# Attention before a routed expert layer: K turned earlier, the row maximum taken off in PSUM, half of K's copy moved to VectorE

## The chip, the cores and the metric

The kernel runs on one core of a Trainium2 chip. PE (TensorE) multiplies matrices, DVE (VectorE) and ACT (ScalarE) do elementwise work and reductions, POOL (GpSimd) issues most transfers and some elementwise work, SP (SyncE) issues others. Each engine works through its own queue in program order and waits on semaphores for the others. The metric is device time in microseconds. Three runs of the kernel before took 343.34, 342.05 and 343.24 us; the median is 343.24.

## The reference

First a chunked attention: 4 batches, 8 heads, 768 positions, 64 columns a head. Each chunk of 32 queries sees 16 positions to its left, itself, 8 to its right, and 8 memory positions: 64 keys. Then a layer of 8 experts in which each row goes to its two best by noisy logits.

```python
for c in range(nc):
    k_full = np.concatenate([mem_k, k_ctx], axis=2)
    v_full = np.concatenate([mem_v, v_ctx], axis=2)
    scores = scale * np.matmul(q_c, k_full.transpose(0, 1, 3, 2))
    scores = scores - np.max(scores, axis=-1, keepdims=True)
    a = np.exp(scores)
    a = a / (np.sum(a, axis=-1, keepdims=True) + 1e-09)
    out[:, :, c_start:c_end] = np.matmul(a, v_full)
...
logits = x @ w_gate
noisy_logits = logits + np.log1p(np.exp(x @ w_noise)) * noise
top2 = np.argpartition(-noisy_logits, 2, axis=1)[:, :2]
...
for e in range(E):
    for k in range(2):
        mask = top2[:, k] == e
        h = np.maximum(x[mask] @ w1[e], 0.0)
        out[mask] += top2_w[mask, k, None] * (h @ w2[e])
```

Taking the row maximum off changes nothing in the quotient as long as the same value is taken off a whole row; it keeps the exponential in range.

## The kernel before

The attention works on 16 pairs of heads (`NPAIR`), one pair in one iteration of a software pipeline (lines 755 to 799). The order of work is written out by hand; nothing reorders it. In iteration i the stages of several pairs are interleaved:

- `PT_pe(i-1)` turns the exponentials P of the pair before on PE, `PT_copy(i-1)` copies them out of PSUM on ACT.
- `max_dve(i)` takes the row maxima of the scores (L288) and subtracts them into an SBUF tile (L290), both on DVE.
- `turn_pe(i+2, 0)` turns Q of a later pair on PE and copies it on ACT (L258); `turn_pe(i+2, 1)`, later in the iteration, does the same with K, whose two heads go in two copies of 64 partitions, both on ACT (L264).
- `PV_pe(i-1)` multiplies P and V on PE (L314, L317), the sums of the rows coming along as a column of ones; `mult_dve(i-1)` takes the reciprocal (L328) and writes the product (L329) on DVE.
- `exp_act(i)` takes the exponential of the subtracted scores on ACT (L295).
- `logits_pe(i-3)` and `xT_pe(i-2)` are the router's matmuls and transposes; `scores_pe(i+1)` writes the next pair's scores.

The scores have one place, two banks of PSUM (`bankS`); the value products have two more (`bankO`). The turned tiles go around three banks (`bankT`): a transpose has to wait until the copy of the tile three places before has read its bank. After every fourth pair the routing of a batch is spread over `steps(...)`: first the gate's exponential and logarithm on ACT, then small operations mostly on DVE (L369 to L470), some matmuls on PE (L407 to L412, L463, L484), one product on POOL (L456), and the gate weights' exponential on ACT (L402). DVE's queue therefore holds, in an iteration: maximum, subtraction, a routing step, reciprocal and product, another routing step. POOL issues the loads of Q and K six pairs ahead (`load_qk`) and of V three pairs ahead (`load_v`), and SP stores the rows that the router has weighted (L422). The expert work begins in the last iterations and follows until about 324 us; scatters on POOL (L676) end the kernel.

Of the kernel before, what the change touches and what calls it, by code (L numbers as in the profile page):

```python
# [12 lines left out]
F32 = mybir.dt.float32  # L13
BF16 = mybir.dt.bfloat16
F32R = mybir.dt.float32r
AX = mybir.AxisListType.X
Alu = mybir.AluOpType
Act = mybir.ActivationFunctionType
# [6 lines left out]
def kernel(  # L25
# [14 lines left out]
    nc = tc.nc  # L40
    B, H, S, D = q.shape
    n_mem = mem_k.shape[2]
    chunk, left_ctx, right_ctx = 32, 16, 8
    ncnk = S // chunk
    scale = 1.0 / math.sqrt(D)
# [6 lines left out]
    BT = S // 128  # L52
    HP = H // 2
    WIN = left_ctx + chunk + right_ctx
    CTX = WIN + n_mem
    SJ = S // 128
    assert D == 64 and CTX == 64 and 4 * chunk == 128 and S == 128 * SJ
    NPAIR = B * HP
# [20 lines left out]
    const = ctx.enter_context(tc.tile_pool(name="const", bufs=1))  # L79
# [9 lines left out]
    def body():  # L89
        actx = ExitStack()  # L90
        ap_ = actx.enter_context(tc.tile_pool(name="ap", bufs=2))
# [4 lines left out]
        bankS = psA.tile([128, 2, 512], F32, name="bankS")  # L96
# [49 lines left out]
        identb = const.tile([128, 128], BF16, name="identb")  # L146
# [21 lines left out]
        for hh in range(2):  # L168
            nc.gpsimd.dma_start(
                out=memv[64 * hh + WIN:64 * hh + CTX, :, hh, 0:D],  # L170
                in_=bass.AP(mem_v.tensor, mem_v.offset + hh * n_mem * D, [[D, n_mem], [2 * n_mem * D, NPAIR], [1, D]]))
# [20 lines left out]

        ident = ap_.tile([32, 32], F32, name="ident", bufs=1)
        nc.vector.tensor_copy(ident, identb[:32, :32])
        onesb = const.tile([128, 128], BF16, name="onesb")
        nc.vector.memset(onesb, 1.0)
        neg = const.tile([128, 2, left_ctx], BF16, name="neg")
        nc.vector.memset(neg, NEG)
        mkT = ap_.tile([128, HP, B, 2, n_mem], BF16, name="mkT", bufs=1)
        nc.vector.memset(mkT, 0.0)  # L200
        kbufs = [ap_.tile([128, 2, S], BF16, name=f"kT{i}", bufs=1) for i in range(2)]
# [44 lines left out]
        st = [dict() for _ in range(NPAIR)]  # L246
        xrows = {}

        def turn_pe(n, x):
            src = qks[n][x]  # L250
            p_t = bf16v(tr(), SJ, 128)
            for j in range(SJ):
                for hh in range(2):
                    nc.tensor.transpose(out=p_t[64 * hh:64 * hh + 64, j, :], in_=src[:, hh, j * D:(j + 1) * D], identity=identb)  # L254
            p_t = p_t.rearrange("d j p -> d p j")
            if x == 0:
                dst = ap_.tile([128, 128, SJ], BF16, name="qT", bufs=2)
                nc.scalar.copy(dst, p_t)  # L258
                st[n]["qT"] = dst.rearrange("d p j -> d (p j)")
            else:  # L260

                for hh in range(2):
                    hs = slice(64 * hh, 64 * hh + 64)
                    nc.scalar.copy(kbufs[n % 2][hs, hh].rearrange("d (p j) -> d p j", j=SJ), p_t[hs])  # L264

        UB = BT // 2

        def scores_pe(n):
            b, hp = divmod(n, HP)
            qT, kT = st[n]["qT"], kbufs[n % 2]  # L270
            ps = bankS[:, :, :UB * 2 * CTX].rearrange("p x (u h c) -> p x u h c", h=2, c=CTX)
            for u in range(BT):
                nc.tensor.matmul(out=ps[:, u // UB, u % UB, :, WIN:], lhsT=qT[:, 128 * u:128 * (u + 1)], rhs=mkT[:, hp, b], start=True, stop=True)
            for c in range(ncnk):
                u, r = divmod(c, 4)
                lo = left_ctx if c == 0 else 0
                hi = WIN - right_ctx if c == ncnk - 1 else WIN
                k0 = chunk * c - left_ctx
                o = ps[32 * r:32 * r + 32, u // UB, u % UB]
                nc.tensor.matmul(out=o[:, :, lo:hi], lhsT=qT[:, chunk * c:chunk * (c + 1)], rhs=kT[:, :, k0 + lo:k0 + hi], start=True, stop=True)  # L280
                for a, z in ((0, lo), (hi, WIN)):
                    if z > a:
                        nc.tensor.matmul(out=o[:, :, a:z], lhsT=onesb[:, :chunk], rhs=neg[:, :, :z - a], start=True, stop=True)  # L283
            st[n]["ps"] = bankS[:, :, :UB * 2 * CTX].rearrange("p x (u c) -> p x u c", c=CTX)

        def max_dve(n):
            mx = ap_.tile([128, 2, BT], F32, name="mx")
            nc.vector.tensor_reduce(out=mx, in_=st[n]["ps"], axis=AX, op=Alu.max)  # L288
            sd = ap_.tile([128, 2, BT, CTX], F32, name="sd", bufs=1)
            nc.vector.tensor_tensor(out=sd, in0=st[n]["ps"], in1=mx.rearrange("p x (u o) -> p x u o", o=1).to_broadcast([128, 2, BT, CTX]), op=Alu.subtract)  # L290
            st[n]["sd"] = sd

        def exp_act(n):
            P = ap_.tile([128, BT, 2, CTX], BF16, name="P")
            nc.scalar.activation(out=P.rearrange("p u h c -> p (u h c)"), in_=st[n]["sd"].rearrange("p x u c -> p (x u c)"), func=Act.Exp, scale=scale)  # L295
            st[n]["P"] = P

        def PT_pe(n):
# [456 lines left out]
        for i in range(NPAIR + 1):  # L755
            if i + NQ < NPAIR:
                load_qk(i + NQ)
            if i >= 1:
                PT_pe(i - 1)
            if i < NPAIR:  # L760
                max_dve(i)
            if i >= 1:
                PT_copy(i - 1)
            if i + 2 < NPAIR:
                turn_pe(i + 2, 0)
            if i < NPAIR:
                steps(1)
            if i >= 1:
                PV_pe(i - 1)
            if i < NPAIR:  # L770
                exp_act(i)
            if i >= 3:
                logits_pe(i - 3)
                if (i - 3) % HP == HP - 1:
                    begin, *rest = route((i - 3) // HP)
                    begin[0]()
                    assert not pending
                    pending.extend(rest)
            if i + 2 < NPAIR:
                turn_pe(i + 2, 1)  # L780
            if i >= 1:
                mult_dve(i - 1)
            if i >= 2:
                xT_pe(i - 2)
            if i + 1 < NPAIR:
                scores_pe(i + 1)
            if 1 <= i <= NPAIR - NV:
                load_v(i + NV - 1)
            if i == 1:
                route_constants()  # L790
            if i == NPAIR - 6:
                load_w1(0)
            if i == NPAIR - 4:
                load_w1(1)
            if i == NPAIR - 2:
                load_w2(0)
            steps(1 if i < NPAIR - 2 else 2)
            if i >= NPAIR - 1:
                units(FB // 2)
# [28 lines left out]
        half = rt.tile([64, E], F16, name="half")  # L828
# [53 lines left out]
    end, past, ovc, ramp, identb, tr, bf16v, f32v, relu, hring, yring, lp, load_w1, load_w2, W1, W2 = kept  # L882


    with tc.For_i(SKIP, end, 128) as i:
# [5 lines left out]
        for t in range(NP):  # L891
# [13 lines left out]
            out=xl, out_offset=None, in_=xd, in_offset=bass.IndirectOffsetOnAxis(ap=gi[:, 0:1], axis=0),  # L905
            bounds_check=N - 1, oob_is_err=True)
        o = lp.tile([128, Dm], F32, name="o")
# [54 lines left out]
```

## Time and profile before

| | |
|---|---|
| median of three runs | 343.24 us |
| time of the profiled execution | 343.07 us |
| span from first to last instruction | 341.3 us |
| busy: PE / DVE / ACT / POOL | 274.3 / 161.2 / 149.5 / 229.3 us |
| mean granted PE clock | 0.918 |
| starts of the sixteen maxima (L288), first and last | 13.6 and 101.3 us |
| row maximum, mean (L288) | 953 ns |
| subtraction, mean (L290) | 958 ns |
| exponential, mean (L295) | 847 ns |
| half copy of K on ACT, mean (L264) | 791 ns |

Busy time is read against a stretch of the span, not against the whole: the attention stage lies between about 10 and 104 us. An engine that is busy nearly all of a stretch bounds it there; idle time of an engine that isn't the bound costs nothing. What an engine waited for stands in brackets behind a row of the order of time, with the line that released it; "issue" there is time in which nothing that the profile shows was waited for. Matmuls are pipelined, and their ends are modelled.

### The profile page before, as it was taken

What the parts mean: (1) busy time and instruction counts of PE and PEld (TensorE: products, weight loads), DVE (VectorE), ACT (ScalarE), POOL (GpSimd) and SP (SyncE); (2) the same over time, 40 slices, a digit from 0 to 9 for tenths busy, and PEclk for the clock granted to TensorE, in tenths of its full rate; (3) what the DMA queues carried; (4) which work ended last, traced back from release to release, by engine and by line L of the source; (5) the groups of instructions that cost most, each with busy time, mean ns of one, the idle gap of its engine ahead of it and who ended that gap; (6) DMA issues with size and microseconds to landing.
All of it is one profiled execution on the core that took longest, in us unless ns stands there. A gap on an engine that the chain in (4) does not pass through costs nothing. (4 is left out here: it accounts for less than half of the span.)

```text
span 341.3 us, 7625 instructions
## 1 busy us (share of the span) xinstructions
PE 274.3 (80%) x3071; PEld 174.2 (51%) x3085; DVE 161.2 (47%) x363; ACT 149.5 (44%) x295; POOL 229.3 (67%) x219
## 2 busy tenths in 40 slices
PE   0777677878548667799999999999999999999900
PEld 0656566666436555345565555555555555455400
DVE  7457659779876465222434333342332633134100
ACT  1688988878355544123343433423423333132200
POOL 8997767737443250687788887887888784848281
PEclk9969978969695999899999999999999999999965
DMA  9999999999979999469999999999999999959395
GB/s 108 161 154 187 167 161 166 212 133 194 196 143 309 398 286 203 79 103 185 247 152 198 172 240 197 239 195 194 206 160 205 216 148 157 147 74 130 40 131 70
DMA packets 99110, 60.30 MB, mean 177 GB/s; under 512 B 63488, under 2 KB 83968, under 8 KB 99072
## 3 DMA queue, kind: packets, MB, share of 16 engines
q0 software_dynamic: 82208, 49.84, 106.5%
q1 hardware_dynamic: 15792, 9.05, 9.2%
q10 hardware_dynamic: 1072, 0.88, 0.8%
q8 instruction: 26, 0.43, 0.5%
q14 instruction: 12, 0.10, 0.1%
HBM read 65.07 MB, written 23.27 MB: 259 GB/s over the span
## 5 line engine op out<-in xcount | busy, mean ns | idle before, releaser
L676 POOL DMA_INDIRECT out_dram<-ys,idx_f x40 | 62.8, 1570 | 26.6 <-issue 14.8
L648 PEld LDWEIGHTS <-w1t 128*128 128x128 bf16 x576 | 56.3, 99 | 40.4 <-issue 5.1
L604 POOL DMA_INDIRECT xl<-x_rows,idx_f x48 | 50.0, 1041 | 26.7 <-DVE hts L633 11.2
L664 PE MATMUL bankE<-w2t,htf 128*128 128x512 bf16 x278 | 65.7, 379 | 0.5
L675 DVE TENSOR_SCALAR ys<-bankE,gt 128x512 f32<-128x512 f32 (+1 forms) x32 | 21.9, 684 | 63.3 <-PE bankE L664 49.8
L648 PE MATMUL bankE<-xTf,w1t 128*128 128x416 bf16 x256 | 50.6, 339 | 0.0
L673 ACT ACTIVATE ys<-bankE,gt 128x512 f32<-128x512 f32 x24 | 16.5, 688 | 68.1 <-PE bankE L664 59.3
L134 POOL DMA_DIRECT2D vp<-in_v_dram x34 | 33.4, 989 | 15.5 <-PE bankO L317 4.3
L664 PEld LDWEIGHTS <-htf 128*128 128x128 bf16 x288 | 27.2, 98 | 28.8 <-issue 0.2
L633 DVE TENSOR_SCALAR htf<-bankE 128x416 bf16<-128x416 f32 x32 | 18.9, 591 | 26.7 <-PE bankE L648 26.7
L631 ACT ACTIVATE htf<-bankE 128x416 bf16<-128x416 f32 x32 | 16.5, 517 | 27.1 <-PE bankE L648 27.1
L264 ACT COPY kT<-bankT 64x768 bf16<-64x768 bf16 x32 | 25.3, 791 | 6.5 <-PE bankT L254 6.2
L648 PE MATMUL bankT<-xTf,w1t 128*128 128x416 bf16 x128 | 27.8, 339 | 0.2 <-DVE htf L633 0.2
L621 PE MATMUL bankT<-identb,xl 128*128 128x128 bf16 (+1 forms) x224 | 20.5, 220 | 5.7 <-DMA xl<-x_rows,idx_f 2.4
L621 PEld LDWEIGHTS <-xl 128*128 128x128 bf16 (+1 forms) x224 | 15.4, 100 | 16.2 <-issue 4.4
L664 PE MATMUL bankE<-w2t,hts 128*128 128x512 bf16 x92 | 22.7, 395 | 0.2
L288 DVE TENSOR_REDUCE mx<-bankS 128x12 f32<-128x768 f32 x16 | 15.2, 953 | 9.1 <-PE bankS L283 9.1
L314 PE MATMUL bankO<-memv,PT 128*128 128x132 bf16 x96 | 10.2, 256 | 9.5 <-ACT PT L307 9.3
L648 PE MATMUL bankE<-xTs,w1t 128*128 128x256 bf16 (+1 forms) x104 | 14.9, 283 | 2.6 <-DVE xTs L625 1.3
L456 POOL TENSOR_TENSOR col<-mm_all,tl 128x672 f16<-128x672 f16 x4 | 6.7, 1672 | 14.6 <-DVE tl L443 14.6
L329 DVE TENSOR_TENSOR xrow<-bankO,rec 128x768 bf16<-128x768 f32 x16 | 15.3, 958 | 1.9 <-DMA x_rows<-xrow 1.4
L290 DVE TENSOR_TENSOR sd<-bankS,mx 128x768 f32<-128x768 f32 x16 | 15.3, 958 | 1.8 <-DVE mx L288 0.5
(182 smaller groups left out, 453.6 us busy)
## 6 DMA issues: line engine op xcount, KB each, us to landing
w1t<-in_moe_w_dram POOLq DMA_DIRECT2D x8, 1024.0 KB, 11.3
w2t<-in_moe_w_dram POOLq DMA_DIRECT2D x8, 1024.0 KB, 10.7
out_dram<-zt SPq DMA_DIRECT2D x3, 2048.0 KB, 10.2
vp<-in_v_dram POOLq DMA_DIRECT2D x30, 168.0 KB, 8.6
qg<-in_q_dram POOLq DMA_DIRECT2D x16, 192.0 KB, 7.7
kg<-in_k_dram POOLq DMA_DIRECT2D x16, 192.0 KB, 8.2
x_rows<-xrow SPq DMA_DIRECT2D x3, 792.0 KB, 8.4
x_rows<-xrow ACTq DMA_DIRECT2D x1, 792.0 KB
```

Source lines behind the costliest of these rows:

```text
L134: nc.gpsimd.dma_start(out=vp[p0 + j:p0 + j + nj, c:c + m, hh, :], in_=bass.AP(v.tensor, v.offset + (hd * S + c * chunk + j - left_ctx) * D ...
L264: nc.scalar.copy(kbufs[n % 2][hs, hh].rearrange("d (p j) -> d p j", j=SJ), p_t[hs])
L290: nc.vector.tensor_tensor(out=sd, in0=st[n]["ps"], in1=mx.rearrange("p x (u o) -> p x u o", o=1).to_broadcast([128, 2, BT, CTX]), op=Alu.s ...
L604: nc.gpsimd.indirect_dma_start(out=xl, out_offset=None, in_=xd, in_offset=bass.IndirectOffsetOnAxis(ap=idx[:, c:c + 1], axis=0), bounds_ch ...
L621: nc.tensor.transpose(out=p_t[:, kp, :w], in_=xl[:w, kp * 64:(kp + 1) * 64].bitcast(BF16), identity=identb[:w, :w])
L631: nc.scalar.activation(out=dst, in_=src, func=Act.Relu)
L633: nc.vector.tensor_scalar(out=dst, in0=src, scalar1=0.0, scalar2=None, op0=Alu.max)
L648: nc.tensor.matmul(out=h[:, :hi - lo], lhsT=W1[e][:, kp, f * 128:(f + 1) * 128], rhs=xTs[s][:, kp, lo:hi], start=(kp == 0), stop=(kp == KP ...
L664: nc.tensor.matmul(out=y, lhsT=ht[:, f, o:o + w], rhs=W2[e][:, f, :], start=(f == 0), stop=(f == FB - 1))
L673: nc.scalar.activation(out=ys[:, :wide], in_=y[:, :wide], func=Act.Copy, scale=gate)
L675: nc.vector.tensor_scalar(out=ys[:, :wide], in0=y[:, :wide], scalar1=gate, scalar2=None, op0=Alu.mult)
L676: ins = nc.gpsimd.indirect_dma_start(out=rows, out_offset=bass.IndirectOffsetOnAxis(ap=idx, axis=0), in_=ys[:, :wide], in_offset=None, bou ...
```

## The change

The change has three parts. K of pair i+2 is turned directly behind Q, right after P's transposes, ahead of the routing step and the value products on PE. The subtraction on DVE goes: DVE writes the maximum as bf16, and behind the value products PE adds it, multiplied by a matrix with -1 on its diagonal, to the scores in PSUM (two matmuls, one a bank); the exponential then reads PSUM. For this the score matmuls open one accumulation a bank, which the two added matmuls close. And of K's two copies the first stays on ACT and the second goes to DVE. A constant, `minus`, is made once.

```diff
--- before.py
+++ after.py
@@ -192,6 +192,8 @@
 
         ident = ap_.tile([32, 32], F32, name="ident", bufs=1)
         nc.vector.tensor_copy(ident, identb[:32, :32])
+        minus = const.tile([128, 128], BF16, name="minus")
+        nc.vector.tensor_scalar(out=minus, in0=identb, scalar1=-1.0, scalar2=None, op0=Alu.mult)
         onesb = const.tile([128, 128], BF16, name="onesb")
         nc.vector.memset(onesb, 1.0)
         neg = const.tile([128, 2, left_ctx], BF16, name="neg")
@@ -259,9 +261,12 @@
                 st[n]["qT"] = dst.rearrange("d p j -> d (p j)")
             else:
 
-                for hh in range(2):
+                def half(copy, hh):
                     hs = slice(64 * hh, 64 * hh + 64)
-                    nc.scalar.copy(kbufs[n % 2][hs, hh].rearrange("d (p j) -> d p j", j=SJ), p_t[hs])
+                    copy(kbufs[n % 2][hs, hh].rearrange("d (p j) -> d p j", j=SJ), p_t[hs])
+
+                half(nc.scalar.copy, 0)
+                half(nc.vector.tensor_copy, 1)
 
         UB = BT // 2
 
@@ -270,29 +275,34 @@
             qT, kT = st[n]["qT"], kbufs[n % 2]
             ps = bankS[:, :, :UB * 2 * CTX].rearrange("p x (u h c) -> p x u h c", h=2, c=CTX)
             for u in range(BT):
-                nc.tensor.matmul(out=ps[:, u // UB, u % UB, :, WIN:], lhsT=qT[:, 128 * u:128 * (u + 1)], rhs=mkT[:, hp, b], start=True, stop=True)
+                nc.tensor.matmul(out=ps[:, u // UB, u % UB, :, WIN:], lhsT=qT[:, 128 * u:128 * (u + 1)], rhs=mkT[:, hp, b], start=(u % UB == 0), stop=False, skip_group_check=True)
             for c in range(ncnk):
                 u, r = divmod(c, 4)
                 lo = left_ctx if c == 0 else 0
                 hi = WIN - right_ctx if c == ncnk - 1 else WIN
                 k0 = chunk * c - left_ctx
                 o = ps[32 * r:32 * r + 32, u // UB, u % UB]
-                nc.tensor.matmul(out=o[:, :, lo:hi], lhsT=qT[:, chunk * c:chunk * (c + 1)], rhs=kT[:, :, k0 + lo:k0 + hi], start=True, stop=True)
+                nc.tensor.matmul(out=o[:, :, lo:hi], lhsT=qT[:, chunk * c:chunk * (c + 1)], rhs=kT[:, :, k0 + lo:k0 + hi], start=False, stop=False, skip_group_check=True)
                 for a, z in ((0, lo), (hi, WIN)):
                     if z > a:
-                        nc.tensor.matmul(out=o[:, :, a:z], lhsT=onesb[:, :chunk], rhs=neg[:, :, :z - a], start=True, stop=True)
+                        nc.tensor.matmul(out=o[:, :, a:z], lhsT=onesb[:, :chunk], rhs=neg[:, :, :z - a], start=False, stop=False, skip_group_check=True)
             st[n]["ps"] = bankS[:, :, :UB * 2 * CTX].rearrange("p x (u c) -> p x u c", c=CTX)
 
         def max_dve(n):
-            mx = ap_.tile([128, 2, BT], F32, name="mx")
+            mx = ap_.tile([128, 2, UB * 2], BF16, name="mx")
             nc.vector.tensor_reduce(out=mx, in_=st[n]["ps"], axis=AX, op=Alu.max)
-            sd = ap_.tile([128, 2, BT, CTX], F32, name="sd", bufs=1)
-            nc.vector.tensor_tensor(out=sd, in0=st[n]["ps"], in1=mx.rearrange("p x (u o) -> p x u o", o=1).to_broadcast([128, 2, BT, CTX]), op=Alu.subtract)
-            st[n]["sd"] = sd
+            st[n]["mx"] = mx
+
+        def shift_pe(n):
+
+            for x in range(2):
+                nc.tensor.matmul(out=bankS[:, x, :UB * 2 * CTX].rearrange("p (g c) -> p g c", c=CTX), lhsT=minus,
+                                 rhs=st[n]["mx"][:, x].rearrange("p (g o) -> p g o", o=1).to_broadcast([128, UB * 2, CTX]),
+                                 start=False, stop=True, skip_group_check=True)
 
         def exp_act(n):
             P = ap_.tile([128, BT, 2, CTX], BF16, name="P")
-            nc.scalar.activation(out=P.rearrange("p u h c -> p (u h c)"), in_=st[n]["sd"].rearrange("p x u c -> p (x u c)"), func=Act.Exp, scale=scale)
+            nc.scalar.activation(out=P.rearrange("p (x u) h c -> p x (u h c)", x=2), in_=bankS[:, :, :UB * 2 * CTX], func=Act.Exp, scale=scale)
             st[n]["P"] = P
 
         def PT_pe(n):
@@ -763,11 +773,13 @@
                 PT_copy(i - 1)
             if i + 2 < NPAIR:
                 turn_pe(i + 2, 0)
+                turn_pe(i + 2, 1)
             if i < NPAIR:
                 steps(1)
             if i >= 1:
                 PV_pe(i - 1)
             if i < NPAIR:
+                shift_pe(i)
                 exp_act(i)
             if i >= 3:
                 logits_pe(i - 3)
@@ -776,8 +788,6 @@
                     begin[0]()
                     assert not pending
                     pending.extend(rest)
-            if i + 2 < NPAIR:
-                turn_pe(i + 2, 1)
             if i >= 1:
                 mult_dve(i - 1)
             if i >= 2:
```

## The prediction

> **What bounds the kernel now.** I first read the page's busy slices: the attention stage (sixteen pairs of heads, about 10 to 104 us) is followed by expert work in which PE is busy nine tenths and more. The chain that ended last holds only closing scatters and says nothing of attention, so I asked for busy time in short windows. The columns are stretch, length, then busy time and instructions of PE, PEld, DVE, ACT, POOL, then granted clock, DMA share and GB/s.
>
> ```profile
> 35.00:40.00 5.00, 3.62 (x104) 2.99 (x104) 3.22 (x5) 4.65 (x7) 3.44 (x4) 1.00 1.95 168
> 76.00:82.00 6.00, 4.84 (x128) 3.82 (x130) 5.62 (x18) 4.99 (x9) 3.58 (x7) 0.90 1.11 162
> 82.00:88.00 6.00, 3.91 (x111) 3.12 (x103) 5.83 (x15) 4.61 (x7) 4.75 (x5) 0.96 1.64 225
> ```
>
> Two regimes: an iteration without routing is ACT's (4.65 of 5.00 us), one with routing on DVE is DVE's (5.62 and 5.83 of 6.00). Next the order of time in a plain iteration, and in a routing one:
>
> ```profile
> 36.12 0.87 ACT L295 ACTIVATE P<-sd 128x768 bf16<-128x768 f32 x1
> 37.30 1.60 ACT L264 COPY kT<-bankT 64x768 bf16<-64x768 bf16 x2 [0.32 <-PE bankT L254]
> 38.92 0.80 ACT L339 COPY xt<-bankT 128x768 bf16<-128x768 bf16 x1
> 39.62 0.80 ACT L307 COPY PT<-bankT 128x768 bf16<-128x768 bf16 x1
> 40.31 0.82 ACT L258 COPY qT<-bankT 128x768 bf16<-128x768 bf16 x1
> ...
> 54.20 0.24 ACT L402 ACTIVATE ge<-gd 128x48 f32<-128x48 f32 x1 [1.26 <-DVE gd L398]
> ...
> 85.26 1.75 DVE L450 TENSOR_TENSOR Rn<-rampm,slot 128x1536 f16<-128x1536 f16 x1
> 87.52 0.94 DVE L288 TENSOR_REDUCE mx<-bankS 128x12 f32<-128x768 f32 x1
> ```
>
> ACT's ring closes in 4.88 us (P's copy before this one began at 34.74, this one at 39.62). The row at 54.20 shows ACT held for a routing operand, with the exponential queued behind it. Then the groups with the prices, count | busy and mean | idle before:
>
> ```profile
> L264 ACT COPY kT<-bankT 64x768 bf16<-64x768 bf16 x32 | 25.3, 791 | 6.5 <-PE bankT L254 6.2
> L290 DVE TENSOR_TENSOR sd<-bankS,mx 128x768 f32<-128x768 f32 x16 | 15.3, 958 | 1.8 <-DVE mx L288 0.5
> L648 PE MATMUL bankE<-xTf,w1t 128*128 128x416 bf16 x256 | 50.6, 339 | 0.0
> ```
>
> and, by the order of time, the nearest small copy on DVE and one of three stalls of PE's queue that nothing in the profile explains:
>
> ```profile
> 50.63 0.32 PE L280 MATMUL bankS<-kT,qT 128*32 128x112 bf16 x11 [1.75 <-issue]
> ...
> 117.75 0.42 DVE L625 COPY xTs<-bankT 128x512 bf16<-128x512 bf16 x1 [1.21 <-PE bankT L621]
> ```
>
> **The change, part by part.** *ACT* loses 16 of 32 K copies: 16 x 0.791 = 12.7 us. The exponential reads PSUM instead of SBUF; the 48-column pair (0.206 from PSUM, 0.242 from SBUF) says no dearer. I take 0.82.
>
> *DVE* loses 16 subtractions (16 x 0.958 = 15.3 us) and gets 16 half copies of K. No row shows a 2-byte copy whose source steps over 128 elements. From below 0.42 to 0.63 us: the 512-element copy as it stands, or scaled by 768/512; from above 0.96, what DVE takes for 768 four-byte elements of PSUM. It is nearest to the latter (768 elements of PSUM that are no neighbours), so 0.95; back to back such DVE operations follow at 0.88 to 0.90. DVE's own work thus stays about equal. What the sum would be at the lower end is rival B below. The Trainium skill's page "VectorE: DVE Perf Modes" (section "What auto-detection actually checks") lets DVE move two 2-byte elements a cycle out of PSUM only where they lie side by side, and so speaks against this change: by it the copy is at its dear end and the sum is the one below. The row of 0.42, whose elements do lie side by side, agrees but can't decide for this copy.
>
> What changes more is DVE's queue. In the changed program's list of instructions, DVE's half carries one wait, on ACT, and none on PE whose transposes it reads; this is only sound if it waits for ACT's half of the same pair. So DVE stands between the maximum and reciprocal, product and routing steps until ACT is through P's copy, Q's copy and its half of K. At the start the second pair's half even lies ahead of the first maximum.
>
> *PE* gets 32 matmuls of 384 columns. One of 416 takes 0.339 from start to end, and 16 of 256 columns follow at 0.12; a pair is so 0.18 + 0.32, about 0.5 us at full clock, 0.85 to 0.95 at half. Their operand repeats each value 64 times; no row shows that at such a width; below, nothing speaks for less than 0.5, above I bound it by twice, 1.0. The nearest repeating rows (166 to 179 ns for 8 to 40 columns) show no surcharge, so 0.5. They lie behind the value products and wait for the maximum; behind them stand logits, transposes and the next scores. The scores now wait for the exponential, not for the subtraction, since it is read from their bank. Flags of the score matmuls: no price, as the value products accumulate likewise. The one new constant on DVE (a row of its size 0.27) hides in front of the first K copy, which can't start before 12.0; without that cover 0.3.
>
> K's transposes move ahead of routing matmuls, value products, logits and the exponential. Their loads are issued 0.7 us behind Q's; Q's transposes waited 0.75 for a load at 29.25, later not. With the later start below, they come at 30.1 or after: nothing, 0.5 without that cover. POOL's value load still waits for the value products; SP's row store follows the routing: no change.
>
> **The new ring.** From the start S of scores: 0.65 scores, 0.55 P transposed, 0.80 P copied, 0.05 + 0.90 value products, 0.53 shift, 0.82 exponential, 0.06, with about 0.05 of friction: 4.41 against 4.88, if DVE's maximum starts by S + 2.0. ACT's K half ends at S + 3.4, so DVE's half starts at S + 3.45, then 0.9, then 1.25 for reciprocal and product, then routing.
>
> **The start.** Old maximum 0 at 13.61. New: ACT's half for pair 1 ends at 16.1, DVE's at 17.1; maximum 18.05, shift, exponential 19.55, scores 1 at 19.6 (16.03 before). P's copy 0 goes from 19.77 to 20.8 (ACT was the brake there), K's half 3 ends at 24.0, product 25.25, the routing constants 1.3: maximum 2 at 26.55 instead of 24.75. Scores 3: 28.95 instead of 27.52, 1.4 late.
>
> **Plain iterations.** Scores 4, 5 and 6 at 33.3, 37.7 and 42.1 (32.65, 37.54, 43.47): 1.4 early.
>
> **Routing.** Iteration 6 ends with 1.75 us of routing on DVE: maximum 7 at 49.45 (51.01). There the exponential stands behind the gate weights, which stand behind K's half and 1.3 us of routing: scores 8 at 53.8 (54.23). K's half in iteration 8 waits for ACT until 57.55 though DVE was free at 56.1; then 0.9 + 1.45 + 1.25 + 1.75: maximum 9 at 62.9 (62.92). The lead is gone. Likewise maximum 11 at 73.25 (74.19), 12 at 79.1 (79.45); DVE then waits for ACT from 80.0 to 81.35; 0.9 + 2.75 + 1.25 + 1.75 + 0.6: maximum 13 at 88.55 (87.52), 1.0 late. After the table work the value products run from 91.2, scores 14 at 93.5, or 94.6 at half clock as before; the middle, and a plain ring: scores 15 at 98.4 (97.53). The last maximum follows the gate's logarithm: 101.85 (101.34). The last shift lies ahead of the first expert matmuls on PE, 0.7 between both clocks: 1.2 us late in all.
>
> **Stalls.** This sum holds no stall of PE's queue; before had three (0.71, 1.75, 0.93 by the idle ahead of their rows), which cost 1.0 + 0.7 + 1.4 = 3.1 us on those marks. Between none and all of them I take half, 1.5, since DVE's waits cover some. The expert stage hands a late start on: PE has under 2 us of any wait in one place there. Total +2.7 on the profiled execution's 343.07 (span 341.3): 345.8, and 345.9 against the median of 343.24, which lies 0.17 above it.
>
> **Rivals.** *A, ACT's relief goes through.* If DVE never makes the ring late, 12 iterations gain 0.47 each: 1.4 + 0.7 - 5.6 = -3.5, 339.6. For it: DVE is idle 19 us in this stage for PE. Against it: the ring stays free only with at most 0.76 us of routing in an iteration, and seven of twelve show 0.7 to 5. The time turns at four of twelve gaining. *B, the half copy is cheap,* 0.42 to 0.63: nine copies lie on the path (three at the start, iterations 7 to 9 and 11 to 13), 0.32 to 0.53 each, 2.9 to 4.8 us less: 341.1 to 343.0. It turns below 0.65. Against it the step of the source; for it only that both are two bytes wide. *C, PE's clock.* PE now stands idle up to 2 us ahead of the table matmuls in iterations 9 and 13; in before it ran at half clock after idle of 0.7 to 1.5 us (43, 57, 71 us). Value products and shift at half clock cost 0.65 + 0.4 each; three iterations more: 349.1. Doubled shift matmuls give about the same.
>
> **Numbers.** My forecast 0.52 (its own range 344 to 348.5), A 0.20, B 0.15, C 0.13. This measurement tells about 0.5% from no change, 1.7 us. Faster: A and a third of B, 0.25; same: the rest of B and the low fifth of mine, 0.20; slower 0.55. For 8 in 10 the range reaches from A's time to C's: 339.3 to 349.3.
>
> **What would show it.** DVE's half of K near 0.95, with DVE idle for ACT ahead of it at about S + 3.45; maximum 2 near 26.5; plain rings near 4.4; maximum 13 near 88.5; the shift pair near 0.5 with the exponential right behind. Wrong: half copies under 0.65, DVE never idle for ACT in iterations 8 and 12, or a clock below before's in the routing iterations.

## The result, and the profile after

The changed kernel took 351.97 us in the median of four runs (350.05 to 352.64), the kernel before 342.64 beside it: a ratio of 1.0269 (95% interval 1.0211 to 1.0327). A later set of runs on another chip gave 1.0325 (1.0272 to 1.0378). It is slower, by about 9 us where 2.7 were forecast, and outside the range. The profiled execution took 352.51 us (span 350.8); the first expert matmul starts at 117.19 us instead of 106.91, so all of the loss arises in the attention stage.

The new prices come first, in the groups of the changed kernel's profile (count | busy, mean ns of one | idle before).

```profile
L266 DVE COPY kT<-bankT 64x768 bf16<-64x768 bf16 x16 | 15.4, 961 | 19.7 <-ACT kT L266 19.6
L266 ACT COPY kT<-bankT 64x768 bf16<-64x768 bf16 x16 | 12.7, 795 | 1.8 <-PE bankT L256 1.8
L305 ACT ACTIVATE P<-bankS 128x768 bf16<-128x768 f32 x16 | 12.9, 809 | 19.7 <-PE bankS L299 19.5
L299 PE MATMUL bankS<-mx,minus 128*128 128x384 bf16 x32 | 9.8, 396 | 3.0 <-DVE mx L293 3.0
```

DVE's half copy of K takes 961 ns against 795 on ACT, and in all DVE stood 19.6 us idle for ACT's half of the same tile. Busy time by stretch in the changed kernel (columns as in the prediction), beside which the prediction shows the same stretches of before:

```profile
35.00:40.00 5.00, 3.58 (x105) 2.83 (x105) 3.53 (x6) 2.96 (x5) 3.76 (x5) 1.00 1.88 175
76.00:82.00 6.00, 4.06 (x106) 3.14 (x106) 5.66 (x13) 3.52 (x7) 4.02 (x5) 1.00 1.53 110
```

ACT fell from 4.65 to 2.96 us of the plain stretch, yet no engine is full there now: between 35 and 40 us PE, DVE and ACT all wait. The order of time of a plain iteration of the changed kernel says for what.

```profile
34.95 0.29 PE L278 MATMUL bankS<-mkT,qT 128*128 128x16 bf16 x6 [0.41 <-ACT P L305]
...
36.20 0.80 ACT L317 COPY PT<-bankT 128x768 bf16<-128x768 bf16 x1 [0.60 <-PE bankT L312]
...
37.58 0.80 ACT L266 COPY kT<-bankT 64x768 bf16<-64x768 bf16 x1
38.41 0.96 DVE L266 COPY kT<-bankT 64x768 bf16<-64x768 bf16 x1 [1.37 <-ACT kT L266]
38.83 0.52 PE L327 MATMUL bankO<-vp,PT 128*32 128x128 bf16 x24 [1.26 <-issue]
39.28 0.50 PE L299 MATMUL bankS<-mx,minus 128*128 128x384 bf16 x2
...
39.82 0.81 ACT L305 ACTIVATE P<-bankS 128x768 bf16<-128x768 f32 x1 [1.44 <-PE bankS L299]
...
40.68 0.29 PE L278 MATMUL bankS<-mkT,qT 128*128 128x16 bf16 x6 [0.41 <-ACT P L305]
...
45.30 0.23 PE L327 MATMUL bankO<-vp,PT 128*32 128x128 bf16 x2 [1.56 <-issue]
```

The iteration before had run from scores at 30.50 to scores at 34.95, 4.45 us, nearly the 4.41 forecast. This one has the same order, but PE stands 1.26 us in the middle of its value products, for nothing that the profile shows, and the ring takes 5.73. The next stall, 1.56, comes at 45.30 and costs more than itself, for PE runs at half speed behind it (a row of six transposes, 0.51 us at 35.59):

```profile
47.79 0.82 PE L312 MATMUL bankT<-identb,P 128*128 128x128 bf16 x6
```

A routing iteration looks like this:

```profile
58.08 0.24 ACT L412 ACTIVATE ge<-gd 128x48 f32<-128x48 f32 x1 [2.68 <-DVE gd L408]
...
59.07 0.29 PE L278 MATMUL bankS<-mkT,qT 128*128 128x16 bf16 x6 [2.32 <-ACT P L305]
...
59.91 0.80 PE L312 MATMUL bankT<-identb,P 128*128 128x128 bf16 x6
...
63.06 0.96 DVE L266 COPY kT<-bankT 64x768 bf16<-64x768 bf16 x1 [1.84 <-ACT kT L266]
...
66.66 1.84 DVE L460 TENSOR_TENSOR Rn<-rampm,slot 128x1536 f16<-128x1536 f16 x1
...
68.43 0.94 DVE L293 TENSOR_REDUCE mx<-bankS 128x12 bf16<-128x768 f32 x1
```

The exponential waits behind the gate weights until 58.23, PE therefore idles 2.32 us, and within a microsecond its transposes run at half speed (0.80 instead of 0.51). DVE's half of K waits 1.84 us for ACT, and product, routing and the next maximum queue up behind it.

The starts of some maxima, in us; "forecast" is the prediction's sum, which holds no stall:

| maximum | 2 | 7 | 9 | 11 | 13 | 15 |
|---|---|---|---|---|---|---|
| before | 24.75 | 51.01 | 62.92 | 74.19 | 87.52 | 101.34 |
| forecast | 26.55 | 49.45 | 62.9 | 73.25 | 88.55 | 101.85 |
| after | 27.32 | 54.77 | 68.43 | 79.16 | 95.19 | 110.98 |

### The profile page after: what moved, and what is told of

Read it like the earlier page. It is cut to its first block, busy times and chain, and to the rows that moved or that the text cites. A ratio compares the mean times of both kernels' runs of the same rounds, so it can differ in the third digit from the quotient of the medians.

```text
span 350.8 us, 7695 instructions
## 1 busy us (share of the span) xinstructions
PE 280.0 (80%) x3103; PEld 177.3 (51%) x3117; DVE 162.8 (46%) x364; ACT 135.5 (39%) x279; POOL 228.8 (65%) x219
## 5 line engine op out<-in xcount | busy, mean ns | idle before, releaser
L266 DVE COPY kT<-bankT 64x768 bf16<-64x768 bf16 x16 | 15.4, 961 | 19.7 <-ACT kT L266 19.6
L674 PE MATMUL bankE<-w2t,hts 128*128 128x512 bf16 x92 | 21.5, 379 | 0.2
L305 ACT ACTIVATE P<-bankS 128x768 bf16<-128x768 f32 x16 | 12.9, 809 | 19.7 <-PE bankS L299 19.5
L317 ACT COPY PT<-bankT 128x768 bf16<-128x768 bf16 x16 | 12.8, 798 | 14.5 <-PE bankT L312 14.5
L293 DVE TENSOR_REDUCE mx<-bankS 128x12 bf16<-128x768 f32 x16 | 15.2, 952 | 5.6 <-PE bankS L288 5.5
L658 PE MATMUL bankT<-xTs,w1t 128*128 128x256 bf16 (+1 forms) x88 | 14.5, 306 | 1.6 <-ACT xTs L633 1.1
```

What stands on the lines that cost most here:

```text
L658: nc.tensor.matmul(out=h[:, :hi - lo], lhsT=W1[e][:, kp, f * 128:(f + 1) * 128], rhs=xTs[s][:, kp, lo:hi], start=(kp == 0), stop=(kp == KP ...
L674: nc.tensor.matmul(out=y, lhsT=ht[:, f, o:o + w], rhs=W2[e][:, f, :], start=(f == 0), stop=(f == FB - 1))
```

## The experiments

Two theories were set against each other. **W**: DVE's half of K waits behind ACT's half and so stands ahead of product and routing in DVE's queue. **R**: the loss is in the longer ring through the one place of the scores, which now runs through PE's shift and takes in PE's stalls and its low clock. The parts are called a (K turned directly behind Q), b (the shift on PE), c (half of K's copy on DVE). The runs were made on several chips, on which the kernel before took 342.05 to 345.49 us in the median; a ratio is always to the kernel before on the same chip, while the expected times went by some 343 us.

**The third part taken back** (a and b stay).

```diff
-                half(nc.scalar.copy, 0)
-                half(nc.vector.tensor_copy, 1)
+                for hh in range(2): ... nc.scalar.copy(...)
```

> The change without its third part: both halves of K's copy on ACT, the turn ahead and the subtraction in PSUM stay. Theory W (the forecast's: DVE's half, queued behind ACT's half, makes DVE late and costs the time): the wait of 19.6 us on DVE goes, the first maximum is back near 13.8 us, plain rings lengthen from 4.45 to about 5.1 us because ACT copies 0.8 us more, routing rings shorten by 1 to 1.5 us; time 343 to 346 us. Theory R (the ring: scores, maximum, shift and exponential now follow one another through one place in PSUM, and PE's stalls and half clock lie on it): the ring stays, only the start gets better; time 348 to 351 us.

342.84 us, ratio 1.0039 (0.9996 to 1.0082), just below W's 343 to 346 and far below R's 348. Without c nothing is left of the loss that could be told from no change. The plain ring is 5.1 us. PE stalls at the very instructions of after, but for 0.18 and 0.82 us instead of 1.26 and 1.56, and once more, 0.74 us, at 82.83: with the slower ring the first two are shorter.

**The second part taken back** (a and c; the subtraction is on DVE again, the shift and its flags are gone).

```diff
+            nc.vector.tensor_tensor(out=sd, in0=st[n]["ps"], in1=mx..., op=Alu.subtract)
...
-                shift_pe(i)
```

> The change without its second part: the subtraction is on DVE again, K turned ahead and half of its copy on DVE stay. DVE then has 15.3 us of subtractions and 15.4 us of half copies. Theory W: the wait for ACT stays and DVE's load grows, slower than the changed kernel, 353 to 358 us. Theory R: scores wait for the subtraction alone, PE's stalls are absorbed again; plain rings near 4.5 us, routing rings DVE's at 6 to 6.5 us, time 344 to 349 us.

347.93 us, ratio 1.0144 (1.0057 to 1.0231): R's figure, and W's is wrong. The subtraction found room in the time in which DVE waited for ACT (that wait fell from 19.6 to 6.2 us), and from maximum 7 to 13 this kernel took 40.55 us, the changed one 40.42. So with c in place, b costs too: some 4 us, which W doesn't explain. The plain ring is 4.18 us, the fastest yet, and its stalls are the longest:

```profile
43.84 0.61 PE L340 MATMUL bankT<-identb,xrow 128*128 128x128 bf16 x4 [3.05 <-issue]
51.40 0.33 PE L283 MATMUL bankS<-kT,qT 128*32 128x112 bf16 x11 [1.11 <-issue]
65.03 0.22 PE L254 MATMUL bankT<-identb,kg 128*64 128x128 bf16 x1 [1.93 <-issue]
```

**The first part taken back** (b and c; K is turned behind the logits again).

```diff
-                turn_pe(i + 2, 1)
...
+            if i + 2 < NPAIR:
+                turn_pe(i + 2, 1)
```

> The change without its first part: K turned behind the logits again, the other two parts stay. K's copies then start later (behind the value products, as before), ACT's half behind the exponential and DVE's half behind that. Theory W: DVE stands longer for ACT, about 1 us more in each of some six rings, 354 to 360 us. Theory R: the ring is not touched by where K is turned, since the transposes fill the time in which PE waits for the exponential: 350 to 353 us. A third reading, that the transposes ahead do the harm because they need a bank that the routing still holds (2.0 us in one iteration): 347 to 350 us.

356.28 us, ratio 1.0406 (1.0321 to 1.0492). As W said: ACT's half now lies behind the exponential, so DVE waits 33.8 us for it. There is no stall of PE at rings of about 5.3.

**The third part alone.**

```diff
+                half(nc.scalar.copy, 0)
+                half(nc.vector.tensor_copy, 1)
```

> The kernel before with the third part alone: K stays turned behind the logits, the subtraction stays on DVE, and the second half of K's copy goes to DVE. W (DVE's half queues behind ACT's half and makes DVE stand in front of the product): here ACT's half lies behind the exponential, so a ring of DVE closes as maximum 0.95, subtraction 0.96, exponential 0.85, ACT's half 0.8, DVE's half 0.95, product 1.25, about 5.8 us against 4.88; over twelve iterations some 8 to 12 us are lost: 350 to 356, and DVE's wait for ACT at K's copy is above 15 us in all. R (the loss comes from the ring through the one place of the scores, which now runs through PE and stalls and a low clock stretch): nothing of that ring is here and ACT is relieved of 12.7 us, so 339 to 343.

365.42 us, ratio 1.0588 (1.0456 to 1.072): W's direction, but beyond its 350 to 356. DVE waits 24.4 us in all for ACT's half, and P's transposes wait 2.82 and 3.01 us (64.82 and 94.08 us) for a bank that DVE's late half still reads, which W hadn't counted. The ring of DVE that W worked out at 5.8 stands in the order of time of this kernel, 5.66 from maximum to maximum:

```profile
39.96 0.95 DVE L291 TENSOR_REDUCE mx<-bankS 128x12 f32<-128x768 f32 x1
...
42.68 0.78 ACT L264 COPY kT<-bankT 64x768 bf16<-64x768 bf16 x1
...
43.49 0.96 DVE L264 COPY kT<-bankT 64x768 bf16<-64x768 bf16 x1 [1.59 <-ACT kT L264]
...
45.62 0.95 DVE L291 TENSOR_REDUCE mx<-bankS 128x12 f32<-128x768 f32 x1
```

ACT lost 12.7 us of work here and the kernel became 20 us slower; c is the harmful part by itself.

**DVE's half put behind the product** (all three parts).

```diff
-                half(nc.vector.tensor_copy, 1)
+                st[n]["k1"] = lambda: half(nc.vector.tensor_copy, 1)
...
+            if i + 2 < NPAIR and i != 13:
+                st[i + 2]["k1"]()
```

> The changed kernel with DVE's half of K's copy issued behind the product of its iteration (in the last iteration but two it stays where it was, because its bank is needed there), and for the second pair behind the first maximum. Nothing else moves. Theory W: DVE no longer stands for ACT ahead of routing and product; the wait of 19.6 us falls under 6, the first maximum is near 13.8 us, maximum 13 comes 3 to 4 us earlier; time 346 to 348.5 us. Theory R: less than 1.5 us is won, all of it at the start; 350 to 352 us.

346.49 us, ratio 1.0109 (1.006 to 1.0158), inside W's expectation: 5.5 us come back when the copy no longer stands ahead of the product. Of its profile, an execution of 350.43 us, only the waits are read: DVE's wait for ACT is down to 2.9 us, and a new one has come, PE for the bank that the late copy still reads:

```profile
71.47 0.58 PE L312 MATMUL bankT<-identb,P 128*128 128x128 bf16 x6 [3.27 <-DVE kT L266]
```

**The shift and the exponential moved up** (a and b, K on ACT; the exponential ahead of K's copies in ACT's queue).

```diff
                 turn_pe(i + 2, 0)
+                shift_pe(i)
+                exp_act(i)
                 turn_pe(i + 2, 1)
```

> The changed kernel with both halves of K's copy on ACT, and with the shift and the exponential put between Q's turn and K's turn, so that the exponential lies ahead of K's copies and of the routing's gate weights in ACT's queue. W (what the first two parts are worth is lost only by where DVE's half and the exponential stand): plain ring 4.85 as ACT's work is, the routing iterations no longer hold the exponential for the gate weights (0.7 to 1.3 us twice), maximum 15 at 97 to 99: 338 to 342. R (a ring that goes through PE's shift is stretched by its stalls and its clock wherever it stands): 342 to 346.

347.52 us, ratio 1.0054 (1.0003 to 1.0104): W's 338 to 342 missed, and by the ratio R's 342 to 346 met. In the profile (an execution of 349.98 us) plain rings took 4.13 us, and behind them PE stalled 1.23, 2.47 and 0.72 us, and 0.96 us at 85.97. By now six kernels of very different order stalled, so PE's matmuls are counted from the start up to each stall. For the two stalls of after (columns as before; PE's count comes first):

```profile
0.00:38.83 38.83, 22.17 (x478) 17.50 (x478) 23.81 (x50) 19.63 (x27) 34.00 (x53) 1.00 1.61 153
0.00:45.30 45.30, 26.50 (x606) 20.87 (x606) 27.46 (x54) 23.32 (x32) 37.72 (x57) 1.00 1.63 157
```

Behind 478 and 606 matmuls, then, 128 apart. Without c: 478, 606, 1373. Without b: 478, 606, 734, 989, 1245. This one: 606, 734, 862, 1374. Before: 606, 734, 989, 1117. All differ from 478 by a multiple of 128, or by one less where a record may be missing. The same holds for every unexplained stall over 0.15 us up to 105 us in all the profiles of this case, 39 of them, and none lies elsewhere. The stalls do not belong to an operation; they stand at fixed places of PE's stream. And each ends 2.2 to 3.4 us behind the start of a transfer of a queue that the page lists under DMA:

```profile
q8 instruction: 26, 0.43, 0.5%
```

26 transfers of some 16 KB for the 6,220 instructions of PE (3,103 matmuls and 3,117 weight loads), about one for 128 matmuls with their loads. In after one started at 35.98 (stall over at 38.83) and one at 42.79 (45.30), in before at 40.04 (43.07) and 47.60 (50.63). So a third theory: **F**, PE's instructions come in blocks, a block is late while the data transfers fill the DMA engines, and a faster ring only reaches the end of its block sooner.

**V's later loads left out.**

```diff
-            if 1 <= i <= NPAIR - NV:
-                load_v(i + NV - 1)
```

> The changed kernel without the loads of V beyond the first four pairs; later pairs are multiplied with the values of earlier ones, so what it leaves out is the transfer of 12 of 16 value tiles. If PE's unexplained stalls at 38.8 and 45.3 us (1.26 and 1.56 us) are refills of its queue that wait for a share of the DMA engines, they shrink to under 0.5 each and maximum 7 comes by 51.5 instead of 54.8; the time is 346 to 350. If they have nothing to do with the transfers, both stay above 1 us and maximum 7 stays at 54 to 55.5, the time at 350 to 353.

One run, 351.23 us. The stalls stand at the same instructions and are half as long, 0.72 and 0.74 us; maximum 7 came at 51.78 instead of 54.77. F's direction, though not the full size expected (under 0.5, by 51.5, and a time of 346 to 350); the last maximum, 111.02, was no earlier than in after, of which below.

**PE kept busy by matmuls that nobody reads.**

```diff
+                nc.tensor.matmul(out=bankL[:, 384:512], lhsT=identb, rhs=onesb, start=False, stop=False, ...)
```

> The changed kernel with matmuls that nobody reads put where PE would stand idle: 12 of 128 columns ahead of the first shift, 8 ahead of each pair's scores (about 0.5 us at full clock, beside the exponential). If PE's low clock at the start (value products and shift at half clock at 22.9 to 25.2 us) and at the end (95 to 107 us) is what came on top of the forecast, it is granted full clock there, maximum 2 comes at 26.0 to 26.6 instead of 27.3, and the time is 347 to 350. If the clock isn't raised by such filling, or costs nothing, the time is 351 to 354.

356.24 us, ratio 1.0359 (1.021 to 1.0507), dearer than expected by either. The clock did rise: value products and shift at the start took 0.52 and 0.50 (0.84 and 0.82 in after), and maximum 2 came at 26.46, the forecast's mark. But the added instructions brought PE sooner to the ends of its blocks: stalls of 1.66, 2.26 and 0.68 us, behind matmuls 478, 734 and 862, the first by now in the middle of other work (scores). That is F again.

**Both kernels without the later loads of Q, K and V**, so that the DMA engines are nearly idle from 27 to 57 us (a share of 0.02 to 0.14 by the busy time in stretches of the changed kernel's cut, 1.6 to 2.1 in after).

```diff
         def load_qk(n):
+            if n >= NQ:
+                qks[n] = qks[n - NQ]
+                return
...
-                load_v(i + NV - 1)
```

> The kernel before without the loads of Q and K from the seventh pair on and of V from the fifth (later pairs work on the tiles of earlier ones); what it leaves out is these transfers. If PE's unexplained stalls are refills of its instructions that take 2.4 to 3.6 us to land while the data transfers fill the DMA engines, the stalls of 0.71, 1.75, 0.42 and 0.93 us go below 0.3 each, and the last maximum comes 1 to 3 us earlier than the kernel before's 101.3: 338 to 342. If the stalls are no matter of the transfers, they stay where they were (43 to 71 us).

> The changed kernel without the same loads. The difference to the same cut of the kernel before is what the change costs without PE's stalls. W (DVE's half waiting behind ACT and standing in front of product and routing is the main loss, the stalls only add about 3 us): the difference is 3 to 6 us, the plain ring is 4.4, maximum 7 comes at 50 to 51.5. R (the loss is the stalls and what they stretch): the difference is under 2 us.

340.38 us (ratio to the kernel before 0.9892, 0.9831 to 0.9954) and 347.27 us (1.0082, 1.0042 to 1.0121). Not one stall over 0.15 us is left in either. The last maximum comes at 98.08 instead of 101.34 in the kernel before (3.26 us, where the prediction had put the cost of its stalls at 3.1) and at 106.22 instead of 110.98 in the changed one (4.76). That settles F's main point: the stalls come with the loads. The transfers of instructions show how: in after the one that follows PE's matmul 478 (38.83) starts at 42.79 and the one that follows 606 (45.30) at 49.08, in the cut PE is at 478 at 37.13 and at 606 at 41.82, and transfers start at 36.76 and 42.68. (POOL's issues go with the loads; the two weren't separated.) But 6.9 us of difference remain between the two cuts, more than W expected, out of 9.3 between the whole kernels: most of the loss is no matter of the stalls. Where they are is seen in one stretch of each, from maximum 7 to 13; the changed kernel's cut first, then that of the kernel before:

```profile
50.65:91.42 40.77, 27.93 (x638) 22.20 (x628) 32.75 (x74) 22.69 (x34) 5.74 (x9) 0.81 0.33 72
```

```profile
49.15:84.30 35.15, 25.74 (x662) 21.14 (x661) 31.58 (x73) 29.36 (x43) 5.74 (x9) 0.90 0.37 84
```

DVE has as much work in both (32.75 and 31.58 us), but idles 8.0 us in the one and 3.6 in the other; 5.3 of the 8.0 are waits for ACT's half of K, three of them. PE's clock is lower, too (0.81 and 0.90).

**The third part taken back, without the loads.**

> The first two parts of the change with both halves of K's copy on ACT, without the same loads. W: without stalls the plain ring is ACT's 5.0 to 5.1, slower than the changed kernel's 4.40, yet the routing iterations are free of DVE's queue: maximum 7 at 52 to 53.5, maximum 15 at 96.5 to 98.5, 338 to 341, that is 6 to 9 us ahead of the changed kernel with the same cut (347.3). If DVE's queue were not the cause, the faster plain ring would leave the changed kernel ahead at maximum 7 by 2 us and both within 2 us at the end.

343.15 us, ratio 0.9962 (0.9928 to 0.9996), so c costs 1.2% or some 4 us without any stall (1.0082 against 0.9962). The expected 338 to 341 and maximum 7 by 53.5 (it came at 54.32) were missed, and so was the lead of 6 to 9 us. But the trade is as W had it: with c the plain ring is 4.40 us, without it ACT's 5.12 (maxima 32.21 and 37.33), which saves c 3.9 us from maximum 2 to 7 (23.33 against 27.23); then from maximum 7 to 13 c takes 40.77 us against 32.47, and loses 8.3. With both halves on ACT, DVE's busy time in that stretch is 26.40 us.

**Filling and no loads together.**

> The changed kernel without the later loads of Q, K and V (what it leaves out are these transfers), and with matmuls that nobody reads where PE would be idle (12 ahead of the first shift, 8 ahead of each pair's scores). Without the loads alone the maxima came at 27.32 (2), 50.65 (7), 91.42 (13) and 106.22 (15), 346 to 348 in time. If PE's half clock is what lay between these marks and the forecast's (26.55, 49.45, 88.55, 101.85), and filling lifts it: maximum 2 by 26.6, maximum 7 by 49.9, maximum 15 by 104; 344 to 346. If the queue on DVE does it by itself, maximum 15 stays at 105.5 to 107 and the time at 346.5 to 349.

347.62 us, ratio 1.0105 (1.0065 to 1.0145): no gain in time. Maximum 2 came at 26.45 and maximum 7 at 49.31, as by the clock theory and 0.14 from the forecast, but the stretch from 7 to 13 took 40.79 us, as without filling, though the clock granted in it rose from 0.81 to 0.89. That speaks for the queue on DVE there. It doesn't rule the clock out, for in the routing iteration PE still idled 1.96 us ahead of the scores at 53.69, and the transposes at 54.71 still took 0.80. The end could not be read, for a reason that the repeat shows.

**The changed kernel once more.**

> The changed kernel once more. If the stalls are refills at fixed places of PE's stream of instructions, the two stalls stand again ahead of the second half of the value products near 38.8 us and ahead of their last two near 45.3 us, together 1.5 to 4 us, maximum 2 comes at 27.3 and maximum 15 at 109 to 112; 350 to 353. If they are chance, they stand at other instructions.

354.66 us, above the 350 to 353 expected (ratio 1.0325). The first stall stands at the same instruction (behind matmul 478), 1.54 us; the second is not there, smaller ones come behind matmuls 350, 734 and 1245 (0.36, 0.54 and 0.28 us). So the places are fixed, but which of them stalls, and for how long, changes from one execution to the next. This time the profile names a releaser for the first:

```profile
38.33 0.52 PE L327 MATMUL bankO<-vp,PT 128*32 128x128 bf16 x24 [1.54 <-DMA vp<-in_v_dram]
```

The V that these matmuls read was loaded by transfers issued at 19.7 us, and loads of V took at most 8.3 us to land in the first 60 us of the changed kernel's first profile; what landed at 38.3 was another pair's, so the name is taken for a coincidence. And a second thing shows, in DVE's waits:

```profile
DVE mx L293 <- remote: 4.3, 1, 4.3
```

Ahead of maximum 14 DVE and ACT both stood for 4 us, for something that the profile lays to no instruction of this core ("remote"). Such a hold of 2.3 to 5.1 us is in all eight profiles taken on two of the chips, with kernels of every kind, and in none on the others. What it is stays open; for this reason late marks are compared only among runs without it.

**A mixture**: pairs 0 to 5 (or 6) as in the kernel before, the later ones with a and b and K on ACT, since the one order is faster in the plain iterations and the other with routing (without loads 32.5 us against 35.2 from maximum 7 to 13).

```diff
+        OLD = 6
...
+            if n < OLD: ... (subtraction on DVE)
...
+                if i >= OLD:
+                    turn_pe(i + 2, 1)
```

> A mixture: pairs 0 to 5 as in the kernel before (subtraction on DVE, K turned behind the logits), pairs 6 to 15 with the first two parts of the change (shift on PE, K turned behind Q) and both halves of K's copy on ACT. By the marks of the runs so far: the kernel before has its maximum 7 at 51.0, the change without the third part then takes 45.0 us from maximum 7 to maximum 15 against 50.3; so maximum 15 at 96 to 97.5, and since the expert stage handed on three quarters of such a lead, 338 to 340.5, below both kernels. If instead what the first two parts win in the routing iterations depends on their slow start, the last maximum comes at 99 or later and the time is 341 to 344.

> The same mixture with pairs 0 to 6 as in the kernel before. Iteration 6 is the first that ends with 1.75 us of routing on DVE, with the subtraction still on it: maximum 7 as in the kernel before at 51.0, the rest as with the boundary at six within 1 us: 338 to 341. If the first routing iteration is what the shift on PE wins most in, it is 1 to 2 us behind the boundary at six.

> The mixture (pairs 0 to 5 as before the change, from pair 6 on the first two parts of it) without the same loads. If its expected lead was given back to refills of PE's instructions: maximum 7 at 49.2, maximum 15 at 94 to 96, against 98.1 of the kernel before with this cut, and 336 to 339 against 340.4. If something else holds it, maximum 15 is at 97 to 98.5 and the time within 1 us of 340.4.

343.30 us (0.9993, 0.9956 to 1.003), 343.18 (0.9985, 0.995 to 1.002) and, without the loads, 339.58 (0.9862, 0.9815 to 0.9909, where the kernel before with that cut had 0.9892), which by the time is the branch "something else holds it". The last maximum of the first came at 98.32, 3 us ahead of the kernel before, but that isn't seen in the time, and the expected 96 to 97.5 and 338 to 340.5 are missed. With loads it stalled 0.87, 1.10 and 1.61 us, the last at 70.68 where the kernel before stalls 0.93. Without the loads maximum 7 came at 50.37, not at 49.2, and maximum 13 at 82.85 (84.30 in the same cut of before), with the hold named above (4.73 us ahead of maximum 14) behind it; so whether refills alone hold it back is not settled. No version beat both kernels.

## Why the prediction was wrong, step by step

*DVE's half copy, 0.95.* Right: 0.961; rival B (0.42 to 0.63) falls. The Trainium skill's page "VectorE: DVE Perf Modes", section "What auto-detection actually checks", had it that DVE moves two 2-byte elements a cycle out of PSUM only where they lie side by side; the trace agrees, with 961 ns for 768 elements that lie 128 apart.

*The shift pair about 0.5, exponential 0.82, ring 4.41.* Right: 0.50 at full clock, 0.81, and rings of 4.45 with loads, 4.40 without. The repeated operand brought no surcharge in these rows.

*One wait, on ACT, with product and routing behind it.* Right in kind, and the main cause. The third part alone costs 20 us, taken back it returns all, moved behind the product 5.5. It isn't c by itself, though: with b taken back and c kept, about half of the loss goes (1.0144 against 1.0269), so R's longer ring has a share. Rival A falls.

*The expert stage hands a late start on.* Right: 10.3 us late there, 9.5 in the span.

*"Between none and all of them I take half, 1.5, since DVE's waits cover some."* This step failed. The sum let the stalls shrink, from before's 3.1 to 1.5; they grew. Taking the loads away brings the last maximum 3.26 us forward in before, close to the 3.1 (though before has a fourth stall, 0.42 us at 64.24, that the prediction left out), and 4.76 in after. After's two stalls idle PE for 2.82 us; the rest goes with them, in part as half speed behind the second. Nothing shows that DVE's waits cover any of it. The prediction had no cause for the stalls and so no reason for half. They are tied to PE's stream of instructions, at every 128th matmul or a multiple, and a faster ring doesn't avoid them. Added up by kernel they are nil at rings of 5.2 us and more, 1.7 us at 5.1, 2.8 in after at 4.45, 6.7 and 5.4 at 4.18 and 4.13; before, with 3.8 at 4.88, falls out of that order.

*The marks at full clock.* This step failed too. Without stalls the last maximum still came 4.37 late (106.22 against 101.85): 0.77 of it at the start, 0.43 by maximum 7, 1.67 from there to maximum 13, 1.50 after. The first two are PE's half clock, for filling brought both marks back (26.45, 49.31). A part of the 1.67 has a row in the routing iteration shown: behind 2.32 us of idle PE the transposes (and in the cut without loads the scores) run at half speed, ACT gets to its half of K later, and DVE's half starts 8.5 us behind maximum 7 instead of 8.1. Filling didn't shorten that stretch, nor lift the clock at that place, so this is a reading and no proof. For the last 1.50, K's transposes wait 1.99 us for the table search in iteration 13, and the matmuls behind them run at half speed (in the cut without loads value products of 0.84 and 0.83 at 94.71 and 95.48, by the next pair 0.52 again; with loads the next pair's, at 104.42, still take 0.84). No run takes this wait away, so the 1.50 isn't shown to come from it. The prediction had this as rival C, for three iterations and 349.1; it came along with the forecast case instead of in its place, from the start on. Its sign, a clock below before's in the routing iterations, shows without the loads (0.81 and 0.90); with them the mean is 0.86 in both kernels from maximum 7 to 13, and after still takes 40.42 us there against 36.51. The page "TensorE: Matmul & The Clock Gate" of the Trainium skill, section "What's actually happening", puts the fall to half clock behind an idle window of about 3.4 us; here 2.3 us without a matmul were enough, and in after the stall of 1.56 us, and the measurement decides.

Together: 4.76 + 4.37 = 9.13 us on the last maximum, of which 1.5 had been allowed for; 3.26 of the 7.63 missing are the stalls, 4.37 the marks. In the time the split is another. Without the loads 6.9 us of difference are left where the sum has 4.3 without stalls (its 1.2 and before's 3.1), and with the loads the stalls add 2.4 more where it let them give back 1.6. Such marks are of one profile each; the changed kernel's repeat was 1.3 us earlier at maximum 13 (93.89). Which of the two steps weighs more is therefore open; both failed, and in the same direction.

## What to carry to other kernels

When work moves to an engine that looks idle, ask first which wait comes with it: a half copy behind the other half ties the second engine's queue to the first, and everything behind it waits too, above all where that engine is the bound. Stalls that "nothing explains" should be counted in instructions of the engine, not in time: here they lay at even distances, which pointed to the supply of instructions, and a faster ring didn't get past them. Terms that the prediction treats as rivals (here low clock and stalls) can all happen at once, and then they add.

## What the runs showed of the hardware that was not expected

PE stalls at fixed places of its instruction stream: 0.2 to 3.05 us, 128 matmuls apart or a multiple of that, while other transfers fill the DMA engines; in the attention stage none over 0.15 us in five kernels without the later loads, nor in two kernels whose rings take 5.2 us or more. That a late block of instructions is the cause is argued from the "instruction" transfers, whose start lies 2.2 to 3.4 us ahead of the end of each stall; shown is that the stalls go with the loads and stand at the count, whatever the operation there. Filling PE's idle time with idle matmuls lifts its clock (0.84 to 0.52 for the value products) but costs instructions, and with busy DMA engines the kernel was no faster for it (1.0359 against 1.0269 and 1.0325 unfilled).
